# A cross-attention block with a locality-gated mixture of experts: token reads in row tiles of 32x128, another order of the attention steps, and scatters declared independent

## The chip, the cores and the metric

The kernel runs on one core of one Trainium2 chip. The metric is device time in microseconds for one execution. Several runs are timed and their median is compared; one further execution is taken by the hardware profiler, and all views of the profile come from that one.

## The reference

```python
# attention: x (8, 8, 512, 64), state (8, 8, 32, 64)
scores = x @ state^T / sqrt(D);   xread = softmax(scores) @ state     # each token reads 32 states
scores2 = state @ x^T / sqrt(D);  sread = softmax(scores2) @ x        # each state reads 512 tokens
x = concatenate([xread, sread], axis=2)      # then heads joined: (8, 544, 512)
# experts: w1 (8, 512, 1024), w2 (8, 1024, 512)
logits = x @ w_gate;  local_gate = sigmoid(x @ w_local)
for b, s in order:                            # per sequence, token by token
    fresh_e = argmax(logits[b, s])
    e = fresh_e if s == 0 or local_gate[b, s] < 0.5 else prev_e
    prev_e = e
    out[b, s] = softmax(logits[b, s])[e] * (relu(x[b, s] @ w1[e]) @ w2[e])
```

Everything is float32. There are 4352 tokens in all (8 sequences of 512 tokens and 32 states), and each goes through one expert, so the work of the second part is that of 4352 rows through two layers, whichever expert each row chooses.

## The kernel before

The kernel has three stages.

**Attention** goes over 8 batches b. The 8 heads of a batch are held as 4 pairs k in groups of 32 partitions, two halves u, so that the scores of one half are one PSUM bank of 128 partitions (4 heads x 32 states) by 512 tokens. For each (b, u): scores on PE (`sc`), maximum over the tokens on DVE (`mx`), 32x32 transposes on DVE (`tr`), maximum over the states (`mo`), subtraction on POOL (`sb`), exponent on ACT (`ex`), sums (`zh` on POOL, `zs` on DVE), the inverse (`zi`), the shares on POOL (`ml`) and the transposes back on DVE (`tb`), which leave the tile `a`: 128 partitions (4 heads x 32 states) by 512 tokens. A second path makes the state reads: exponents over tokens on ACT (`et`), a turn on PE (`tu`), its copy (`ec`), the products with x (`sr`), their scaling (`st`), and a write to the DRAM tensor `rows` (`ws`). Logits for tokens (`lg`, `lt`) and for states (`rt`, `sl`, `sk`) go to the tile `lt`.

The *token reads* (`vv`, L432) multiply the shares by the states. Here the states of four heads were spread into `sd`, a block-diagonal tile of 128 partitions by 256 columns per (b, u), by four ACT copies (`sd`, L268) over a tile cleared on POOL (L220). A step is one (b, chunk of 128 tokens): two matmuls with a contraction of 128 partitions and 256 columns into one PSUM bank, an ACT copy (`xr`, L438) to an SBUF tile of 128x512, and a write of 256 KB to `rows` (`wr`, L446). There are 32 such steps. The pool `p` of four PSUM banks serves token reads, turns, state reads and logits in turn.

The order of all these steps is written out by hand in the string `STEPS`: each name is a step, its digits the batch and the half or chunk. Every engine executes its instructions in the order in which they are issued there. `go` marks where the list pauses and the routing goes on; at each call of `reads()` inside the routing, the steps up to the next `go` are issued.

**Routing** finds the expert of every token (`choose`, L521 to L527; the step `ch` does batches 0 to 6 at once, and the routing itself does the last batch), carries the choice along each sequence with a scan (L557), counts tokens by expert, and gives each token a slot. ACT makes `less` (L607), `behind` (L612) and `end8` (L619) for DVE on the way. The result is `two` (L716), the first two blocks of tokens, then `tok` and `row` for all blocks. A small POOL DMA (`seen`, L719) reads one element of each batch's rows and so waits for all writes to `rows`. Then POOL gathers the first rows (`y`, L827).

**Experts** handles pairs of blocks (256 tokens of one expert) with a seven-product scheme in both layers, 16 pairs in this data, and 9 small tiles of 32 tokens. For each pair u, PE computes 7 products of the first layer (L1013) and 7 of the second (L1053). POOL gathers the rows of later pairs by quarters (L821), each behind a one-element copy (`tick`, L835) that sets the moment, and scatters the two finished blocks y0 and y1 to the output with indirect DMAs (L996). Both scatters write the tensor `out_dram`. The last pairs are issued by `last`, which branches on the number of pairs found at run time.

Of the kernel before, what the change touches and what calls it, by code (L numbers as in the profile page):

```python
# [150 lines left out]
sc0 kp3 xt11 xt10 mx00 ga kp2 sd3 tr01 xt21 mx01 sd2 mo01 nb0 tr00 et01 sb01 xn0 mo00 wm14 sc1 et00 sb00 ex01  # L151
iv0 tu01 tr11 gl tu00 zh01 ex00 tr10 xt20 ec00 zh00 zs01 mo10 sd0 xn1 zs00 sb10 zi0 ec01 mx11 sd1 sr0 ml01 mo11
ex10 mx10 sc2 ml00 st0 xt30 tb01 rt0 sb11 tb00 sl0 xt31 tr20 lg0 nb1 ex11 zh10 sk0 tr21 vv03 et10 zh11 xt41 zs10
vv00 et11 lt0 mx21 xr03 xt51 zs11 tu11 zi1 xr00 tu10 iv1 ml11 mo21 vv02 xt50 ec10 mo20 ml10 sc3 ec11 tb11 xt40
xr02 mx20 sb21 sr1 tb10 xn2 tr30 sb20 ex21 lg1 mx30 st1 vv12 zh21 ex20 rt1 tr31 nb2 sl1 zh20 et20 vv10 zs21 sk1
lt1 ws1 zs20 et21 tu20 zi2 xt60 mo30 xr10 ml20 sc4 xr12 iv2 mx31 ec20 xn3 ml21 tu21 tb20 vv11 mx41 ec21 nb3 sb30
et30 tb21 sr2 tr40 et31 xt61 lg2 mo31 ex30 tu30 mo40 sb31 st2 sc5 lt2 wr00 xr11 mx40 ec30 zh30 tr41 wr03 tu31
ex31 nb4 zs30 sb40 vv23 et40 mx50 xt70 ec31 mo41 tu40 zh31 ex40 rt2 sr3 sb41 zs31 ws0 xr23 zi3 xn5 et41 iv3 sl2
ml31 mx51 vv22 ex41 sk2 iv4 st3 ml30 tb31 sc6 xr22 rt3 ec40 zh41 tb30 xt71 sl3 zh40 zs41 lg3 tr50 nb5 vv31 wr02
zs40 et50 zi4 vv01 xn4 lt3 xr31 ml40 mo50 sk3 tr51 xr01 vv13 ml41 tb40 et51 vv21 mo51 sb50 xr13 wr10 iv5 vv20  # L160
tb41 xr21 sb51 xn6 mx60 ex50 lg4 mx61 xr20 zh50 tu50 ex51 lt4 tu41 tr60 nb6 ec50 zh51 tu51 zs50 et60 mo60 vv32
wr20 ec51 zs51 sb60 zi5 tu60 ec41 wr23 tr61 sc7 xr32 ml50 wr11 ex60 mo61 sr4 et61 ml51 tb50 wr12 mx71 sr5 sb61
ws2 st4 tb51 ec60 ws3 vv30 tr70 zh60 ex61 xn7 mx70 st5 lg5 zh61 xr30 zs60 tu61 mo70 nb7 et70 vv40 zs61 sb70 zi6
ec61 tu70 lt5 wr22 iv6 xr40 ml61 rt5 sr6 rt4 ex70 tr71 wr40 ec70 ml60 mo71 sl5 et71 wr13 sl4 sk5 tb61 vv41 sb71
st6 wr31 tb60 tu71 zh70 ex71 sk4 iv7 wr32 lg6 rt6 xr41 zs70 zh71 sl6 ec71 lt6 wr21 vv42 zs71 zi7 wr01 sr7 sk6
xr42 ml71 ch0 wr42 vv33 st7 ml70 wr41 vv50 tb71 xr33 wr33 tb70 vv53 xr50 rt7 wr30 lg7 xr53 sl7 lt7 wr53 vv51 sk7
go wr50 vv43 xr51 wr51 go xr43 vv52 wr43 vv61 xr52 ws4 vv60 wr52 xr61 go ws5 xr60 vv62 wr60 go xr62 ws7 wr62
vv71 wr61 vv72 xr71 wr71 vv63 xr72 wr72 vv70 xr63 go wr63 go xr70 wr70 ws6 go vv73 xr73 wr73
# [3 lines left out]
class Attention:  # L172


    def __init__(self, ctx, tc, p, late, xn, xt, st, stt, wgl, wgs, lt, rows, none):
# [14 lines left out]
        self.sttc = [once.tile([P, n, KT, N], F32, name=f"sttc{i}") for i, n in enumerate((1, B - 1))]  # L190
# [3 lines left out]
        self.states_of = once.tile([P, B * G * DH], F32, name="states_of")  # L194
        nc.sync.dma_start(out=self.states_of, in_=st)
        nc.sync.dma_start(out=self.sttc[1], in_=stt[:, 1:])
        nc.sync.dma_start(out=wgs.rearrange("p w k e -> p (w k e)"), in_=wgl)
# [3 lines left out]
        self.sd = late.tile([P, B, G * GD], F32, name="sd", bufs=1)  # L201
# [10 lines left out]
    def clear(self):  # L212
        nc = self.nc
        for z in self.zh:
            nc.vector.memset(z[:, :, N // 2:], 1e-9)
        for z in self.z2:
            nc.vector.memset(z[:, :, 1:], 1e-9)
        nc.gpsimd.memset(self.gl, 0.0)
        nc.gpsimd.memset(self.lt, 0.0)
        nc.gpsimd.memset(self.sd, 0.0)  # L220
        nc.gpsimd.memset(self.none, 0.0)
# [8 lines left out]
    def reads(self):  # L230
# [7 lines left out]
                  sd=self.diagonal, ga=self.gates, gl=self.gates_kept, ch=self.choose, kp=self.keep, wm=self.warmed)  # L238
# [23 lines left out]
    def choose(self, i):  # L262
        self.route.choose(self.lt, 0, B - 1)

    def diagonal(self, k):
        r = slice(32 * k, 32 * k + 32)
        to = self.sd[r].rearrange("p b (g d) -> p b g d", g=G)
        self.nc.scalar.copy(to[:, :, :, DH * k:DH * k + DH],  # L268
                            self.states_of[r].rearrange("p (b g d) -> p b g d", b=B, g=G))

    def load_t(self, b, h):
        x = self.new(self.xp, f"x_t{h}", (b,), [P, KT // 2, S])
        self.nc.sync.dma_start(out=x.rearrange("p k s -> p (k s)"), in_=self.xt[b][:, h * D * 2:(h + 1) * D * 2])

# [4 lines left out]
    def states(self, b):  # L279
        return self.sttc[b > 0][:, b - (b > 0)]  # L280
# [147 lines left out]
    def token_reads(self, b, c):  # L428
        v = self.of["v", b, c] = self.bank()
        for u in range(G):  # L430
            d = slice(u * GD, u * GD + GD)
            self.nc.tensor.matmul(v[:, d], lhsT=self.get("a", b, u)[:, c * P:c * P + P], rhs=self.sd[:, b, d],  # L432
                                  start=True, stop=True)

    def reads_kept(self, b, c):
        xr = self.new(self.late, "xr", (b, c), [P, D], bufs=12)
        v = self.get("v", b, c)
        self.nc.scalar.copy(xr.rearrange("p (k u d) -> p u k d", k=KT, u=G),  # L438
                            v.rearrange("p (u k d) -> p u k d", u=G, k=KT))

    def reads_to_rows(self, b, c):
# [3 lines left out]
        t = b * T + c * P  # L445
        self.nc.sync.dma_start(out=self.rows[t:t + P].rearrange("t q x -> t (q x)"), in_=self.get("xr", b, c))  # L446


class Routing:
# [65 lines left out]
    def choose(self, lt, b0, b1):  # L515
# [5 lines left out]
        nc.vector.memset(lt[0:1, b0:b1, 0, E:E + 1], -1.0)  # L521
        nc.vector.tensor_reduce(self.mx[:, c].rearrange("p c o -> p (c o)"), lf[:, :, :E], axis=AX, op=Alu.max)
        nc.vector.tensor_tensor(self.eq[:, c], lf[:, :, :E], self.mx[:, c].to_broadcast([P, n, E]), op=Alu.is_lt)
        nc.vector.scalar_tensor_tensor(self.eq[:, c], self.eq[:, c], float(2 * E), up.to_broadcast([P, n, E]),
                                       Alu.mult, Alu.add)
        nc.vector.tensor_reduce(self.own[:, c], self.eq[:, c], axis=AX, op=Alu.min)
        nc.vector.scalar_tensor_tensor(self.top[:, c], lf[:, :, E], 0.0, self.own[:, c], Alu.is_lt, Alu.mult)  # L527

    def route(self, bank, lt, slots, reads, rows):
# [12 lines left out]
        self.choose(lt, B - 1, B)  # L542
# [239 lines left out]
def experts(ctx, late, tc, bank, w1, w2, rows, slots, route, routing, out):  # L782
# [35 lines left out]

    def quarter(to, k, i):
# [55 lines left out]
    class Tile:  # L875
# [48 lines left out]
        def scatter(self, y):  # L924
            at = bass.IndirectOffsetOnAxis(ap=slots.row[:, self.k, self.q:self.q + 1], axis=0)
            nc.gpsimd.indirect_dma_start(out=out.rearrange("n (q x) -> (n q) x", q=Q), out_offset=at, in_=y,
                                         in_offset=None, bounds_check=NT * Q - 1, oob_is_err=False)
# [66 lines left out]
    def scatter(b, y):  # L994
        to = bass.IndirectOffsetOnAxis(ap=slots.tok[:, b:b + 1], axis=0)
        nc.gpsimd.indirect_dma_start(out=out, out_offset=to, in_=y, in_offset=None, bounds_check=NT - 1,  # L996
                                     oob_is_err=False)
# [232 lines left out]
```

## Time and profile before

| quantity | value |
|---|---|
| median of 3 runs (lowest to highest) | 550.07 us (545.01 to 551.1) |
| the profiled execution's own time | 546.65 us |
| its span, first to last instruction | 544.9 us |
| mean granted clock of PE | 0.987 |
| busy: PE, DVE, POOL, ACT | 524.6, 382.5, 313.0, 174.0 us |
| bytes moved | 155.48 MB, 285 GB/s on average |
| first expert matmul of PE, last matmul's end | 95.08, 535.15 us |

Busy times are sums over the span; a share says little here because the three stages have different limits. In a line of a timeline, the first number is the start in microseconds from the first instruction, the second the length, then the engine, the line of the kernel, the operation, the output and inputs and the number of instructions; square brackets give idle time before it and what ended that. PEld is PE's weight load. A line of a group gives busy time and the mean of one instruction in ns, and behind the second bar the idle time before the group.

### The profile page before, as it was taken

The page shows a single profiled execution, that of the slowest core. Times are in us where ns is not written, and L with a number is a line of the kernel's source. Part 1 is how long each engine was busy: PE and PEld are TensorE (multiplying, and loading weights), DVE is VectorE, ACT ScalarE, POOL GpSimd, SP SyncE. Part 2 cuts the span into 40 slices and gives each one's busy share as a digit, 9 for nine tenths or more (in the row PEclk, how much of TensorE's full clock was granted, in tenths as well). Part 3 has the DMA queues.
Part 4 walks back from the last instruction along what each step waited for, and adds up shares of the span by engine and source line. Part 5 has one row for each costly group of instructions (what it writes and reads, how often), then busy time and mean ns, then how long its engine had stood idle before and what let it go on. Part 6 is the DMA issues. An engine that isn't in the chain of part 4 may idle for free. (4 is left out here: it accounts for less than half of the span.)

```text
span 544.9 us, 12958 instructions
## 1 busy us (share of the span) xinstructions
PE 524.6 (96%) x4916; PEld 459.3 (84%) x4916; DVE 382.5 (70%) x623; ACT 174.0 (32%) x359; POOL 313.0 (57%) x386
## 2 busy tenths in 40 slices
PE   8799898999999999999999999999999999999992
PEld 2567766989989898989898989899999998999992
DVE  6999876738575667575756658495776777777763
ACT  6788654111313232222222222223222221322230
POOL 7788602655574567565655556446565655445555
PEclk9999998999999999999999999999999999999997
DMA  8999766799989898898989898874748475565742
GB/s 320 410 350 350 294 237 214 275 397 390 377 284 387 299 376 322 327 369 299 375 294 369 293 366 299 320 251 142 259 142 302 134 276 178 216 218 205 248 151 99
DMA packets 49003, 155.48 MB, mean 285 GB/s; under 512 B 6865, under 2 KB 8017, under 8 KB 45602
## 3 DMA queue, kind: packets, MB, share of 16 engines
q1 hardware_dynamic: 41234, 135.78, 68.5%
q0 software_dynamic: 7552, 18.69, 9.6%
q8 instruction: 42, 0.69, 0.5%
q14 instruction: 31, 0.25, 0.1%
q10 hardware_dynamic: 144, 0.07, 0.1%
HBM read 136.68 MB, written 17.89 MB: 284 GB/s over the span
## 5 line engine op out<-in xcount | busy, mean ns | idle before, releaser
L821 POOL DMA_INDIRECT xg<-rows,row x132 | 157.4, 1192 | 29.5 <-issue 27.3
L930 DVE TENSOR_TENSOR a<-a,a 128x1024 f32<-128x1024 f32 x64 | 77.0, 1223 | 31.2 <-DMA a<-in_w_dram 29.8
L1013 PE MATMUL ps<-xt,a 128*128 128x128 f32 x720 | 88.6, 276 | 0.0
L1013 PE MATMUL sum<-xs,a 128*128 128x128 f32 x720 | 87.7, 275 | 0.0
L1013 PEld LDWEIGHTS ps<-xt,a 128*128 128x128 f32 x720 | 84.4, 192 | 2.1 <-issue 1.8
L1013 PEld LDWEIGHTS sum<-xs,a 128*128 128x128 f32 x720 | 84.0, 192 | 0.0
L930 DVE TENSOR_TENSOR c<-c,c 128x1024 f32<-128x1024 f32 x64 | 75.4, 1219 | 3.7 <-DMA c<-in_w_dram 3.2
L1053 PE MATMUL ps<-c,h 128*128 128x256 f32 x312 | 74.7, 382 | 0.0
L1053 PEld LDWEIGHTS ps<-c,h 128*128 128x128 f32 x312 | 58.0, 190 | 10.9 <-issue 3.7
L996 POOL DMA_INDIRECT out_dram<-y,tok x32 | 35.0, 1093 | 52.8 <-issue 16.8
L1053 PE MATMUL ps<-c,hs 128*128 128x256 f32 x256 | 60.5, 379 | 0.0
L1053 PEld LDWEIGHTS ps<-c,hs 128*128 128x128 f32 x256 | 48.6, 190 | 6.6
L1053 PE MATMUL sum<-c,h 128*128 128x256 f32 x200 | 47.2, 379 | 0.0
L930 DVE TENSOR_TENSOR h<-s,s 128x512 f32<-128x512 f32 x15 | 10.4, 693 | 51.5 <-ACT s L1036 48.2
L1053 PEld LDWEIGHTS sum<-c,h 128*128 128x128 f32 x200 | 38.0, 190 | 5.2
L849 DVE STREAM_TRANSPOSE xt<-xg 128x512 f32<-128x512 f32 x32 | 34.2, 1091 | 8.4 <-DMA xg<-rows,row 8.4
L964 ACT COPY sum<-ps 128x256 f32<-128x256 f32 (+1 forms) x31 | 14.3, 460 | 71.1 <-PE ps L1013 49.5
L835 POOL COPY tick<-s 1x1 f32<-1x1 f32 x45 | 15.9, 354 | 36.3 <-ACT s L1036 36.3
L835 POOL COPY tick<-r 1x1 f32<-1x1 f32 x41 | 17.2, 419 | 30.5 <-ACT r L1058 22.9
L432 PE MATMUL p<-sd,a 128*128 128x256 f32 x128 | 32.1, 390 | 0.2 <-ACT xr L438 0.2
L1058 ACT ACTIVATE r<-sum,prob 128x256 f32<-128x256 f32 x32 | 15.1, 473 | 52.0 <-PE sum L1053 49.5
L1053 PE MATMUL sum<-c,hs 128*128 128x256 f32 x128 | 30.2, 379 | 0.0
(230 smaller groups left out, 757.8 us busy)
## 6 DMA issues: line engine op xcount, KB each, us to landing
a<-in_w_dram SPq DMA_DIRECT2D x68, 512.0 KB
c<-in_w_dram SPq DMA_DIRECT2D x68, 512.0 KB
at<-in_w_dram SPq DMA_DIRECT2D x18, 1024.0 KB
ct<-in_w_dram SPq DMA_DIRECT2D x18, 1024.0 KB
x_t<-in_xt_dram SPq DMA_DIRECT2D x16, 512.0 KB
x_n<-in_xn_dram SPq DMA_DIRECT2D x8, 1024.0 KB
rows<-xr SPq DMA_DIRECT2D x32, 256.0 KB
xg<-rows,row POOLq DMA_INDIRECT x132, 5.7
```

The lines of the kernel that those rows point to most:

```text
L432: self.nc.tensor.matmul(v[:, d], lhsT=self.get("a", b, u)[:, c * P:c * P + P], rhs=self.sd[:, b, d], start=True, stop=True)
L821: nc.gpsimd.indirect_dma_start(out=to.rearrange("p x k -> p (x k)"), out_offset=None, in_=rows.rearrange("n q x -> (n q) x"), in_offset=ba ...
L835: nc.gpsimd.tensor_copy(tick, value)
L849: nc.vector.transpose(to.rearrange("p k (i t) -> p k i t", i=Q), xgs_[u % 2][:, b].rearrange("p i x k -> p k i x"))
L930: nc.vector.tensor_tensor(out, a, b, op=op)
L964: nc.scalar.copy(y, x)
L996: nc.gpsimd.indirect_dma_start(out=out, out_offset=to, in_=y, in_offset=None, bounds_check=NT - 1, oob_is_err=False)
L1013: nc.tensor.matmul(to[:, m * P:m * P + P], lhsT=w[:, j, m * P:m * P + P], rhs=x[:, j, :], start=begin and m == 0 and j == 0, stop=(m == FK ...
L1053: nc.tensor.matmul(to, lhsT=x[:, m, :], rhs=w[:, m, :], start=begin and m == 0, stop=(m == FK // 2 - 1), skip_group_check=True)
L1058: nc.scalar.activation(to, t, Act.Copy, scale=p)
```

## The change

Six things change.

1. A token-read step is now a whole batch. The tile `sd`, its memset and its four copies go; the states are used as loaded, 32 partitions and 64 columns for each head. Each head pair k has a PSUM bank of its own, so one step takes all four banks of the pool `p`; it issues 32 matmuls of 32 partitions x 128 stationary columns by 64 moving columns. Four ACT copies of 128x512, one for each bank, fill one SBUF tile, and one DMA writes 1 MB to `rows`.
2. The order in `STEPS` is new throughout.
3. The choice of batches 0 to 6 is issued as five steps, `ca` to `ce`, with other steps between them, behind the last logits.
4. The initial loads are split: the states of batch 1 (`la`) before the others (`lb`).
5. The scatters to the output are declared independent of one another, for pairs and for small tiles.
6. In the last pairs, the fourth quarter of the gather that goes with the second layer is issued only behind the branch, when another pair follows.

```diff
 STEPS = """   (the end of the list)
-st6 wr31 tb60 tu71 zh70 ex71 sk4 iv7 wr32 lg6 rt6 xr41 zs70 zh71 sl6 ec71 lt6 wr21 vv42 zs71 zi7 wr01 sr7 sk6
-xr42 ml71 ch0 wr42 vv33 st7 ml70 wr41 vv50 tb71 xr33 wr33 tb70 vv53 xr50 rt7 wr30 lg7 xr53 sl7 lt7 wr53 vv51 sk7
-go wr50 vv43 xr51 wr51 go xr43 vv52 wr43 vv61 xr52 ws4 vv60 wr52 xr61 go ws5 xr60 vv62 wr60 go xr62 ws7 wr62
-vv71 wr61 vv72 xr71 wr71 vv63 xr72 wr72 vv70 xr63 go wr63 go xr70 wr70 ws6 go vv73 xr73 wr73
+sl3 tu61 mo71 et71 ws5 sk3 zs70 sb71 wr3 ex61 iv7 tu71 iv6 ec61 rt5 zh61 sl5 ex71 sr6 sk5 ec71 zs61 zh71 zi6 sr7
+ml61 zs71 st6 zi7 ws6 rt6 ml60 sl6 st7 tb61 ws7 sk6 rt7 vv2 ml71 tb60 ml70 tb71 xr23 xr21 tb70 xr20 xr22 sl7 lg6
+wr2 sk7 lg7 lt6 ca lt7 cb vv6 cc cd ce xr63 go xr62 xr60 go xr61 vv5 wr6 xr53 xr51 go xr50 xr52 go wr5 vv4 xr43
+xr41 xr40 xr42 vv7 wr4 go go xr73 xr72 xr70 go xr71 wr7
...
-        for u in range(G):
-            d = slice(u * GD, u * GD + GD)
-            self.nc.tensor.matmul(v[:, d], lhsT=self.get("a", b, u)[:, c * P:c * P + P], rhs=self.sd[:, b, d],
-                                  start=True, stop=True)
+        v = self.of["v", b] = [self.bank().rearrange("p (c u d) -> p c u d", c=SC, u=G) for k in range(KT)]
+        for c in range(SC):
+            for u in range(G):
+                for k in range(KT):
+                    r = slice(32 * k, 32 * k + 32)
+                    self.nc.tensor.matmul(v[k][:, c, u, :], lhsT=self.get("a", b, u)[r, c * P:(c + 1) * P],
+                                          rhs=self.states_of[r, b, u, :], start=True, stop=True)
...
+    def reads_kept(self, b, k):
+        xr = self.new(self.late, "xr", (b,), [P, SC, KT, G * DH], bufs=3)
+        self.nc.scalar.copy(xr[:, :, k, :], self.get("v", b)[k].rearrange("p c u d -> p c (u d)"))
...
+        self.nc.sync.dma_start(out=self.rows[t:t + S].rearrange("(c t) q x -> t c (q x)", c=SC),
+                               in_=self.get("xr", b).rearrange("p c k x -> p c (k x)"))
...
+    def apart(scatter):
+        tc.declare_no_dep(scatter.ins, group="scatters", reason="a token has one slot, so scatters write other rows")
+        tc.add_to_no_dep_group("scatters", scatter.ins)
...
+        rest = gets[1]
+        if not late:
+            calls = iter(range(NP))
+            gets[1] = lambda value: rest(value) if next(calls) < Q - 1 else None
...
-        pair(u, u + 1 < NP, waiting=waiting, late=False)
+        rest = pair(u, u + 1 < NP, waiting=waiting, late=False)
         if u + 1 < NP:
             with tc.If(pairs > u + 1):
+                rest()
                 last(u + 1)
```

## The prediction

> **What bounds the kernel now.** I read the busy time by stage first, then the line of time inside each stage, then the groups, then the chain that ended last.
>
> Busy time in five stages: columns are the stretch, its length, busy time and instructions of PE, PEld, DVE, ACT and POOL, granted clock, DMA share, GB/s.
>
> ```profile
> 8.05:57.26 49.21, 44.63 (x913) 30.18 (x915) 46.80 (x110) 41.28 (x93) 39.23 (x50) 1.00 0.98 374
> 57.26:69.45 12.19, 10.84 (x211) 8.92 (x200) 10.58 (x33) 6.77 (x16) 6.37 (x7) 1.00 0.75 276
> 69.45:95.08 25.63, 22.81 (x169) 16.40 (x168) 18.12 (x58) 13.05 (x31) 2.96 (x3) 0.92 0.65 227
> 95.08:535.15 440.07, 440.07 (x3619) 402.14 (x3616) 300.04 (x405) 109.27 (x210) 253.23 (x311) 1.00 0.79 284
> 535.15:544.90 9.75, 0.00 (x0) 0.00 (x0) 2.75 (x3) 0.00 (x0) 4.51 (x4) 0.65 0.23 76
> ```
>
> Attention, 8.05 to 69.45: DVE works 57.4 of 61.4 us, so DVE sets it, not PE. Routing, 69.45 to 95.08: a chain of small steps over DVE, PE and ACT. Experts, 95.08 to 535.15: PE without a gap at the full clock; the pairs with a small tile repeat every 28.73 us. Nothing there can be gained by an edit that takes no matmul away, and the change takes none. What is left to move is the start of the experts and the 9.75 us after PE's last matmul.
>
> The line of time gives the links that I use:
>
> ```profile
> 9.55 1.19 PEld L289 LDWEIGHTS p<-wgs,sttc 64*32 64x32 f32 x128 [1.29 <-DMA wgs<-in_wg_dram]
> 61.93 0.35 DVE L363 RECIPROCAL z<-z 128x32 f32<-128x32 f32 x1
> 62.20 1.10 PE L390 MATMUL p<-x_n,e 128*32 128x64 f32 x64
> 62.42 2.26 POOL L367 TENSOR_TENSOR e<-e,z 128x512 f32<-128x512 f32 x2 [1.00 <-DVE lt L521]
> 69.28 0.17 DVE L527 SCALAR_TENSOR_TENSOR top<-lt,own 128x5 bf16<-128x5 f32 x1
> ...
> 78.49 0.15 ACT L619 COPY end<-ps 8x2 f32<-8x2 f32 x1 [0.17 <-PE ps L617]
> 78.99 0.22 DVE L627 TENSOR_SCALAR past<-iof,end 8x23 bf16<-8x23 f32 x1
> 83.42 0.83 POOL L719 DMA_DIRECT2D seen<-rows  x1 [18.74 <-DMA rows<-xr]
> 85.03 0.95 PEld L710 LDWEIGHTS <-inp 128*128 128x128 bf16 x16 [0.15 <-DVE inp L686]
> 88.17 0.16 DVE L716 TENSOR_TENSOR two<-high,ps 128x2 int32<-128x2 f32 x1
> 89.39 1.17 POOL L827 DMA_INDIRECT y<-rows,two  x1 [5.13 <-DMA a<-in_w_dram]
> ```
>
> The last choice (L527) ends at 69.45, ACT's copy end8 (L619) lets DVE go on at 78.99, `two` is ready at 88.33, the gather of the first rows goes out at 89.39 and PE begins at 95.08. POOL's `seen` shows when the last row has landed: 83.4, five us ahead of need.
>
> The groups by shape, for the part that is rewritten:
>
> ```profile
> L432 PE MATMUL p<-sd,a 128*128 128x256 f32 x128 | 32.1, 390 | 0.2 <-ACT xr L438 0.2
> L390 PE MATMUL p<-x_n,e 128*32 128x64 f32 x512 | 8.9, 220 | 3.4 <-DMA x_n<-in_xn_dram 2.9 <-issue 0.5
> L438 ACT COPY xr<-p 128x512 f32<-128x512 f32 x32 | 18.6, 586 | 9.5 <-PE p L432 8.6 <-ACT others L634 0.9
> ```
>
> The tail, POOL in order of time, and then the piece of the chain that lies between the two scatters:
>
> ```profile
> 535.04 1.02 POOL L996 DMA_INDIRECT out_dram<-y,tok  x1 [0.30 <-issue]
> 536.03 0.81 POOL L835 COPY tick<-y 1x1 f32<-1x1 f32 x1
> 537.00 1.80 POOL L821 DMA_INDIRECT xg<-rows,row  x1 [0.16 <-issue]
> 540.07 1.02 POOL L996 DMA_INDIRECT out_dram<-y,tok  x1 [1.27 <-DMA out_dram<-y,tok]
> ```
>
> ```profile
> 535.04 4.20 DMA out_dram<-y,tok
> ```
>
> **The change, part by part.** *Scatters (tail).* The second scatter of the last pair waits for the first to land and has a tick and a gather before it. Both go. Its data (L1080) is ready at 535.66, so it starts at 535.04 + 1.02 + 0.30 = 536.36 in place of 540.07: -3.7. The two 256 KB scatters then travel together; scatters took 3.2 to 10.2 us to land in this trace, so I give 0.3 back: **-3.4**, bounds -2.0 and -3.7. The same wait vanishes in the other pairs, where PE's 440 us cover it (POOL idled up to 7.8 us there and PE not at all). The deferred gather goes out after the branch, still some 15 us ahead of its transpose: nothing. Without that cover DVE's L849 would wait, as it does now for 8.4 us in all.
>
> *Work taken off PE, ACT and POOL in attention.* Gone: the 3.5 us memset of `sd`, four ACT copies of 1.04, and most of the 32.1 us of L432. DVE waited for PE 2.2 us in the whole stage, 1.0 of it really for the load of the second x_t; ACT and POOL are below it. So nothing directly: DVE's own 57.4 us cover it.
>
> *The new order on DVE.* The instructions are the same; only waits can change. Head: the second batch's x_t comes after the same bytes, so its wait (12.4 to 13.35) stays. x_n of batch 0 moves behind three x_t halves, and the maxima of batch 2 come before it is used: 0 to +0.9. Middle: 1.2 us of small waits, of which some may close. End: now POOL makes the last shares (62.42 to 64.68) while DVE runs the 3.4 us choice of batches 0 to 6 (62.24 to 65.73). The change puts that choice behind the last logits, so its cover is gone: the four shares of 1.05 follow one another on POOL and DVE has a 0.6 us transpose between them, three waits of 0.4; and the sums of the second half of batch 6 wait 0.7 for subtract, exponent and halves. From the last score transpose to the last choice I count 2.7 us of waits in place of 1.6: +1.1. Together I take **+0.6** (end +1.1, half a us back in the middle), bounds -2.8 (all 4.0 us of idle gone but the 1.2 of the load) and +2.0.
>
> *Token reads as a serial chain.* Let P be PE's time for one batch: 64 loads and 64 passes of 64 columns, in four row tiles. A batch takes all four banks of the pool, so the next cannot begin before the four copies (0.54 apart) are done. In the order issued, 17 of 32 copies were done by the last reciprocal before; after, 12. Batches 5, 4 and 7 now stand, one after the other, ahead of the matmul of `ends` on PE and, 5 and 4, of `less` on ACT. From the end of the last choice c: the exponent waits for DVE (0.5) and takes 0.5, the fourth copy of batch 6 ends at c + 1.6; batch 5: 0.2 + P + 0.25 + 2.1; batch 4 the same; batch 7: 0.2 + P; `ends` and end8 0.7. With P = 1.1: c + 10.9, where now it is 78.99 - 69.45 = 9.5. **+1.3**, and three times every us that P is longer. DVE waits there, and behind it the slots, `two`, the gather and PE's first matmul.
>
> P itself no row shows. Below: 1.10 us for the 64 records of L390, four column tiles side by side (0.93 without start-up). Above: loads that do not overlap, 0.95 / 16 = 59 ns each (L710), 64 of them 3.8 us. L289 decides: 128 loads of 32 columns in 1.19 us are 9.3 ns each, less than a quarter of 59, so loads into different tiles do run together. I take 1.1.
>
> The Trainium skill (TensorE: Matmul & The Clock Gate, LDWEIGHTS) says that a load's time goes by columns and that 32x128 costs as much as 128x128, which speaks against four times as many loads. No run here shows it for row tiles; taken alone it would give the serial 3.8 us and the slow case below.
>
> PE's clock: granted 0.50 from 88 to 90 us although PE shows busy, after two us of four-column matmuls. With fewer matmuls in routing that can come earlier; P would be 2.2 and the sum 3.3 us more.
>
> *Rows.* 32 writes of 256 KB become 8 of 1 MB on SP, the last after the last copy (c + 13.2) instead of at 81.32 = c + 11.9; 0.75 MB more at 380 GB/s adds 2 us to the 2.1 that it took to land: c + 17.4. `two` comes at c + 20: covered by 2.6 us, beyond which every us counts. The first expert's loads stand behind it on SP and meet the gather: **+0.3**, bounds 0 and 1. On SP the row writes of five batches move behind all loads of x, which then land earlier; that is part of the lower bound on DVE, and 22 issues of 0.33 us fewer on a queue that nobody waits for are worth nothing. Four more warming matmuls lie in PE's idle 14.3 to 17.1, the extra load on SP behind full DMA queues: nothing.
>
> Sum: -3.4 + 0.6 + 1.3 + 0.3 = -1.2. The profiled execution took 546.65 (span 544.9 and 1.75 around it) and would take 545.4; the median of the runs is 550.07, 3.4 above it, so I forecast **548.9**. Runs of before spread over 1.1%, so about 1% (5.5 us) is what can be told from no change; this is within.
>
> **The rivals.** *Row tiles that do not run together.* P = 3.8, from serial loads; the chain is 3 x 2.7 = 8.1 longer: 548.9 + 8.1 = 557.0. For it: 128 columns a load, no row of this form. Against it: L289. Slower at all from P = 1.5, by over 1% from P = 3.3.
>
> *The order closes DVE's waits.* -2.8 on DVE, P = 0.93 (chain +0.8), no collision, tail -3.7: -5.7, 544.4. For it: the idle is there and PE, ACT and POOL are relieved. Against it: the lost cover at the end, which I could follow link by link.
>
> *The scatters gain nothing,* because the second meets the first on its way: +3.4, 552.3. Against it: the 4.2 us are a wait and not a transfer.
>
> **How the numbers follow.** Forecast 0.44, with its own range 546 to 552.5; serial tiles, or a cold clock added to other losses, 0.27; waits closed 0.25; scatters without gain 0.04, which is within 1% too. So faster by over 1% 0.25, within 0.48, slower 0.27. The range 543.5 to 557.5 takes in both rivals' times with a little beyond.
>
> **What would show it.** Tail: the last two scatters 1.3 us apart, some 6 us from PE's end to the span's. Token reads: 64 records in about 1.1 us. Routing: DVE's step behind end8 (now L627) at c + 10.9. DVE: idle before the last transposes; the last choice near 70. Experts: 440 us as before. I am wrong if PE's first expert matmul comes before 95 or after 101, or if the stretch of experts itself changes.

## The result, and the profile after

The changed kernel takes 575.74 us (median of 4 runs, 572.47 to 578.24) against 550.59 us (4 runs, 545.01 to 552.39): the ratio is 1.0471, with a 95% interval of 1.0374 to 1.0569. Here and below a ratio leaves out executions more than 1.5% above the fastest of the same kernel, while a median takes in all. The kernel is slower by 25 us, and the forecast of 548.9 us with its range up to 557.5 is wrong.

The profiled execution took 578.24 us, its span is 576.4 us. Its busy time by stage, columns as in the prediction (length, PE, PEld, DVE, ACT, POOL, granted clock, DMA share, GB/s):

```profile
8.04:57.26 49.22, 39.88 (x956) 25.45 (x954) 43.77 (x98) 31.18 (x75) 36.42 (x47) 0.90 0.93 342
57.26:77.71 20.45, 17.11 (x373) 14.81 (x373) 13.03 (x44) 9.70 (x24) 9.05 (x10) 0.68 0.50 190
77.71:113.59 35.88, 31.70 (x341) 24.90 (x337) 18.21 (x57) 14.96 (x36) 3.11 (x3) 0.64 0.55 193
113.59:569.69 456.10, 452.00 (x3619) 404.43 (x3616) 300.51 (x405) 109.42 (x210) 248.97 (x311) 1.00 0.76 275
569.69:576.40 6.71, 0.00 (x1) 0.00 (x0) 2.75 (x3) 0.00 (x0) 1.73 (x1) 0.77 0.16 54
```

The last choice now ends at 77.71, PE's first expert matmul starts at 113.59, its last ends at 569.69. Before, these were 69.45, 95.08 and 535.15. Two things stand out against the stages of before: the granted clock is 0.64 to 0.90 up to the experts (it was 1.00, and 0.92 in routing), and PE is idle for 4 us in the experts, where it had no gap. By links of the chain:

| link | before | after | difference | forecast |
|---|---|---|---|---|
| last choice ends | 69.45 | 77.71 | +8.3 | +0.6 |
| from there to DVE's step behind end8 | 9.5 | 19.4 | +9.9 | +1.3 |
| from there to the first expert matmul | 16.1 | 16.4 | +0.3 | +0.3 |
| experts | 440.1 | 456.1 | +16.0 | 0 |
| PE's end to the end of the span | 9.75 | 6.7 | -3.0 | -3.4 |

The sum is +31.5 us, which is the difference of the two spans. The medians are 25 us apart: the profiled execution is the slowest of the four of after, and that of before lies below its median.

Some token reads on PE in order of time: one in attention, three in routing (seven matmuls of the first of these stand outside its row of 57), then the matmul of `ends` and the DVE step that waits for its copy.

```profile
53.02 2.01 PE L434 MATMUL p<-states_of,a 32*128 32x64 f32 x64
81.37 3.46 PE L434 MATMUL p<-states_of,a 32*128 32x64 f32 x57 [0.16 <-ACT xr L439]
86.66 4.24 PE L434 MATMUL p<-states_of,a 32*128 32x64 f32 x64
91.62 5.14 PE L434 MATMUL p<-states_of,a 32*128 32x64 f32 x64 [0.72 <-ACT xr L439]
97.15 0.23 DVE L641 TENSOR_SCALAR past<-iof,end 8x23 bf16<-8x23 f32 x1 [3.32 <-ACT end L633]
```

A read takes 2.01 us where the clock is 1.00 and 3.5 to 5.1 us in routing. The same view cut at the steps of the granted clock shows why:

```profile
30.56:40.80 10.24, 9.89 (x117) 5.70 (x116) 8.25 (x18) 6.89 (x17) 8.32 (x11) 0.50 1.00 389
57.87:68.11 10.24, 8.82 (x142) 7.29 (x146) 5.57 (x19) 6.00 (x15) 4.73 (x7) 0.50 0.64 244
74.93:102.24 27.31, 24.62 (x278) 19.95 (x279) 14.30 (x53) 9.64 (x26) 0.00 (x0) 0.50 0.50 185
```

For 47.8 us ahead of the experts PE has half its clock, although it counts as busy for nine tenths of that time. The first stretch begins as the first read ends (28.04 to 30.57), and in the third 18.4 of PE's 24.6 busy us are reads. Ahead of the second PE had also been idle, from 56.49 to 59.29, so that stretch need not come from the reads alone. Who waited for whom in attention (total, times, longest):

```profile
DVE lt L425 <- PE p L421: 5.8, 4, 3.3
DVE nb L314 <- PE s L306: 5.0, 4, 2.8
PE p L389 <- issue: 2.8, 1, 2.8
PE p L421 <- issue: 1.7, 1, 1.7
```

The same view of before has 0.8 us for the first row and 0.2 us for the second. DVE, which set attention before, now waits for PE, and twice PE itself waited for nothing that the trace shows ("issue"). The tail does what was forecast. Its last scatter starts as soon as its data is there:

```profile
567.14 1.03 POOL L1015 DMA_INDIRECT out_dram<-y,tok  x1 [0.30 <-DVE y L1092]
570.57 1.73 POOL L1015 DMA_INDIRECT out_dram<-y,tok  x1 [2.41 <-DVE y L1099]
```

The 16 us in the experts lie in the pairs with a small tile. One of them, in order of time:

```profile
163.75 1.01 POOL L945 DMA_INDIRECT out_dram<-yt,row  x1 [0.30 <-issue]
163.89 1.01 PEld L923 LDWEIGHTS ps<-at,xtt 128*32 128x32 f32 x23
163.89 3.63 PE L923 MATMUL ps<-at,xtt 128*32 128x256 f32 x32
165.06 1.33 POOL L840 DMA_INDIRECT xgt<-rows,row  x1 [0.30 <-issue]
165.48 0.15 PEld L923 LDWEIGHTS ps<-at,xtt 128*32 128x32 f32 x4 [0.57 <-issue]
166.21 0.17 PEld L923 LDWEIGHTS ps<-at,xtt 128*32 128x32 f32 x4 [0.58 <-issue]
```

The first 23 weight loads come as before, then four at a time with 0.57 us between them, again for no reason that the trace shows; the 32 matmuls take 3.63 us, where before they took 1.93. Nearly all of the 16 us is here: 13.8 in these matmuls of the tiles' first layer (10.0 busy and 3.8 idle), some 2 in those of their second. POOL issued the tile's scatter 0.14 us ahead of them. Before, it came behind them, because it waited for the pair's scatters to land.

### The profile page after: what moved, and what is told of

Read it like the earlier page. It is cut to its first block, busy times and chain, and to the rows that moved or that the text cites. A ratio compares the mean times of both kernels' runs of the same rounds, so it can differ in the third digit from the quotient of the medians.

```text
span 576.4 us, 13666 instructions
## 1 busy us (share of the span) xinstructions
PE 547.1 (95%) x5302; PEld 471.3 (82%) x5302; DVE 379.9 (66%) x623; ACT 168.9 (29%) x355; POOL 302.5 (52%) x383
## 4 chain that ended last, share of the span: by engine, by line
PE 82%; issue 2%; DVE 1%; ACT 1%; DVEq 0%
PE ps L1072 22%; PE ps L1032 19%; PE sum L1032 14%; PE sum L1072 12%; PE ps L923 5%; PE ps L935 3%; PE ps L1116 3%; PE ps L724 2%; PE p L434 2%; PE ps L551 1%; ACT xr L439 0%; DVE a L949 0%; PE ps L875 0%; PE sum L551 0%; DVE oh L584 0%
## 5 line engine op out<-in xcount | busy, mean ns | idle before, releaser
L840 POOL DMA_INDIRECT xg<-rows,row x131 | 151.4, 1156 | 36.3 <-issue 36.1
L949 DVE TENSOR_TENSOR a<-a,a 128x1024 f32<-128x1024 f32 x64 | 76.8, 1221 | 15.3 <-DMA a<-in_w_dram 13.9
L1072 PEld LDWEIGHTS ps<-c,h 128*128 128x128 f32 x312 | 58.0, 190 | 10.9 <-issue 3.7
L854 POOL COPY tick<-r 1x1 f32<-1x1 f32 x41 | 11.6, 282 | 86.5 <-ACT r L1077 83.2
L1015 POOL DMA_INDIRECT out_dram<-y,tok x32 | 37.6, 1174 | 26.1 <-DVE y L1099 14.4
L434 PEld LDWEIGHTS p<-states_of,a 32*128 32x128 f32 x512 | 28.2, 271 | 5.3 <-ACT xr L439 3.6
L434 PE MATMUL p<-states_of,a 32*128 32x64 f32 x512 | 30.1, 365 | 1.2 <-ACT xr L439 0.9
L923 PE MATMUL ps<-at,xtt 128*32 128x256 f32 x288 | 27.4, 385 | 3.8 <-issue 2.4
```

The lines of the kernel that those rows point to most:

```text
L434: self.nc.tensor.matmul(v[k][:, c, u, :], lhsT=self.get("a", b, u)[r, c * P:(c + 1) * P], rhs=self.states_of[r, b, u, :], start=True, stop ...
L840: nc.gpsimd.indirect_dma_start(out=to.rearrange("p x k -> p (x k)"), out_offset=None, in_=rows.rearrange("n q x -> (n q) x"), in_offset=ba ...
L854: nc.gpsimd.tensor_copy(tick, value)
L923: nc.tensor.matmul(hps[SQ * g:SQ * g + SQ, :], lhsT=self.x_t[:, j, :], rhs=a[:, j, :, g], start=(j == 0), stop=(j == KT - 1))
L949: nc.vector.tensor_tensor(out, a, b, op=op)
L1015: apart(nc.gpsimd.indirect_dma_start(out=out, out_offset=to, in_=y, in_offset=None, bounds_check=NT - 1, oob_is_err=False))
```

## Experiments

Two theories at the start. *A:* the time before the experts goes to the row-tile reads, by their length on PE and by the clock that they bring down; the time in the experts goes to scatters that now meet the tiles' matmuls. *B:* the reads are innocent, the new order makes the chain long, and the experts suffer from something else, such as PE's longer program. The runs come from five chips; every ratio is against the kernel before on the same chip, and that kernel's own median went from 545.45 to 550.92 us between chips.

### First chip: the parts apart

scatters_alone: the kernel before with parts 5 and 6 of the change and nothing else.

```diff
-        nc.gpsimd.indirect_dma_start(out=out, out_offset=to, in_=y, in_offset=None, bounds_check=NT - 1,
-                                     oob_is_err=False)
+        apart(nc.gpsimd.indirect_dma_start(out=out, out_offset=to, in_=y, in_offset=None, bounds_check=NT - 1,
+                                           oob_is_err=False))
...
+            calls = iter(range(NP))
+            gets[1] = lambda value: rest(value) if next(calls) < Q - 1 else None
```

> The kernel before with the independent scatters and the gather deferred behind the branch, and nothing else of the change. Theory A: a small tile's scatter, no longer held back by the landing of the pair's scatter, goes out some 0.3 us ahead of the tile's first-layer matmuls and slows their issue; 2 us a tile, 8 tiles of 9. The stretch of experts 452 to 456 us in place of 440, the tail 6.7 us in place of 9.75, the time some 10 to 13 us above the kernel before. Rival R: the experts are slow in the changed kernel because PE's program is longer and its code comes later, not because of scatters. Experts 440 us, tail 6.7, the time 3 us below the kernel before.

Measured: 560.03 us, ratio 1.0191 (1.0146 to 1.0236). First expert matmul at 94.55, experts 456.7 us, tail 6.65. So the loss in the experts comes with the scatters (the deferred gather concerns only the last pairs, which have no tile), without any other part of the change.

scatters_undone: the changed kernel without those two parts.

```diff
-            apart(nc.gpsimd.indirect_dma_start(out=out.rearrange("n (q x) -> (n q) x", q=Q), ...))
+            nc.gpsimd.indirect_dma_start(out=out.rearrange("n (q x) -> (n q) x", q=Q), ...)
...
```

> The changed kernel with the scatters dependent on one another again and the last gather where it was. Theory A: first expert matmul at 113 to 114 us as in the changed kernel, experts 440 us, tail 9.8, the time some 563 to 566, 12 below the changed kernel. Rival R: experts still 456 us; only the tail comes back, the time 3 us above the changed kernel.

Measured: 566.49 us, ratio 1.0267 (1.0201 to 1.0332). First expert matmul at 111.6, experts 444.3 us. The two halves of the loss separate, as A has it: the tiles' first layer is back at 17.4 us, as in the kernel before. Some 4 us above 440 remain, most of them in the tiles' second layer (20.0 us busy and 0.8 idle, where before it took 17.6).

wide_reads: the changed kernel with the old form of the reads.

```diff
-        v = self.of["v", b] = [self.bank().rearrange("p (c u d) -> p c u d", c=SC, u=G) for k in range(KT)]
...
+        v = self.of["v", b] = [self.bank() for c in range(SC)]
+        for c in range(SC):
+            for u in range(G):
+                d = slice(u * GD, u * GD + GD)
+                self.nc.tensor.matmul(v[c][:, d], lhsT=self.get("a", b, u)[:, c * P:c * P + P], rhs=self.sd[:, b, d], ...)
```

> The changed kernel with the token reads as they were: a block-diagonal tile, two matmuls of 128 partitions by 256 columns for each chunk, in the new order, four banks a batch. Theory: the row tiles are what makes PE slow and lowers its granted clock (0.50 from 75 to 102 us), and that delays DVE's last choice too. Then the clock stays at 1.00 in attention, the last choice ends at 70 to 73 us, the first expert matmul comes at 95 to 99, the experts stay slow by 16 us, the time is 557 to 562. Rival: the new order itself makes the choice late and the chain behind it long; last choice at 75 or later, first expert matmul at 105 or later, the time 567 or more.

Measured: 576.24 us, ratio 1.0485 (1.0424 to 1.0546). Last choice at 79.97, first expert matmul at 110.83. My expectation failed: as a whole the old form is no better in this order. But the clock behaves as A has it. While the same three reads stand at the same place of the chain, PE keeps its full clock:

```profile
80.00:102.60 22.60, 18.83 (x113) 12.96 (x114) 14.55 (x48) 12.43 (x33) 0.21 (x1) 1.00 0.61 210
94.69 0.23 DVE L648 TENSOR_SCALAR past<-iof,end 8x23 bf16<-8x23 f32 x1 [1.90 <-ACT end L640]
```

A wide read of a whole batch takes 3.72 us at the full clock. From the last choice to DVE's step behind end8 the chain takes 14.7 us with three of those: 5.2 more than before, 4.7 less than the 19.4 with row tiles at half clock. Most of that is lost again before: beside scatters_undone, which has the row tiles on the same chip, the last choice comes 3.6 us later (76.4 there) and the first expert matmul 0.8 sooner. In attention the clock is not the row tiles' alone, since this run has it at half for some 10 us between 20 and 60 us. Both parts count: an order that puts whole batches into the chain, and a form that loses the clock. (The four block-diagonal copies of ACT, which I placed, cost DVE 1.9 us as well; so this run does not price the order alone.)

rows_in_turn: the same matmuls, one row tile after the other.

```diff
-        for c in range(SC):
-            for u in range(G):
-                for k in range(KT):
+        for k in range(KT):
+            for c in range(SC):
+                for u in range(G):
```

> The changed kernel with the 64 matmuls of a token read in another order: all 16 of one row tile, then the next row tile, in place of four tiles side by side. If loads into different row tiles overlap, this takes the overlap away: a batch goes from 2.0 us at the full clock to 3 or more, and the time grows by 4 to 8 us. If they run one after the other already, a batch stays at 2.0 us (4 to 5 at half clock) and the time within 3 us of the changed kernel.

Measured: 626.11 us, ratio 1.1401 (1.133 to 1.1472); a read takes up to 11.5 us at half clock in place of 4.2:

```profile
119.23 11.53 PE L434 MATMUL p<-states_of,a 32*128 32x64 f32 x64
```

So row tiles side by side do overlap, by a factor of 2.7 (11.53 / 4.24, both at half clock). The Trainium skill (TensorE: Matmul & The Clock Gate, Packing small matmuls) gives 3.07 for four row tiles with 512 columns; with 64 columns this case comes near it, with 2.7. My rival of tiles that do not run together is refuted.

### Second chip: place, form, order, clock

tile_scatter_late: scatters_alone, with the tile's scatter meant to be issued later.

```diff
-            strassen(u, others, gets[0], waiting)
+            strassen(u, others, gets[0], waiting[:2])
...
+        for results in waiting[2:]:
+            results()
```

> The kernel before with the independent scatters and the deferred gather, as scatters_alone, but each small tile's scatter is issued on POOL behind the gather of the next tile, some 2.3 us later, when the tile's first-layer matmuls are nearly over. Theory: it is the scatter's coincidence with the tile's matmuls that costs 2 us a tile. Then the tile's 32 first-layer matmuls take 1.9 us again, experts 440 to 444 us, tail 6.7, the time 546 to 550, at or 3 us below the kernel before. Rival: independent scatters cost PE the same wherever they lie; experts 452 or more, the time 556 or more.

Measured: 543.75 us, ratio 0.9958 (0.9933 to 0.9983), experts 440.5 us. The edit proved to be empty: a pair has only two results waiting, and both stayed where they were, so these are the instructions of scatters_alone in the same order, on another chip. There the same program lost 16 us, here nothing. The loss in the tiles belongs to some chips (no chip was used a second time, so a cause that lasts only as long as one stay on a chip is not excluded).

plain_tile_writes: scatters_alone with a plain write to a scratch tensor in place of the tile's scatter; the kernel leaves out the small tiles' rows of the output.

```diff
-            apart(nc.gpsimd.indirect_dma_start(out=out.rearrange("n (q x) -> (n q) x", q=Q), out_offset=at, in_=y, ...))
+            nc.gpsimd.dma_start(out=spare[self.i * P:self.i * P + P], in_=y)
```

> As scatters_alone, but each small tile's result goes out by a plain DMA of the same 64 KB, issued by POOL at the same place, to a scratch tensor; the rows of the small tiles in the output are left out. If any write issued there slows PE, the experts stay at 454 to 457 us and the time at 558 to 561. If it is the indirect form (POOL working out an address for every row) they come back to 440 to 444 us and the time to 547 or so.

Measured: 544.75 us, ratio 0.9968 (0.9941 to 0.9995), experts 441.1 us. Inconclusive, since on this chip the indirect form loses nothing either.

rows_old_order: row-tile reads in the order of before, a batch at a time, with the scatters dependent as before (one stretch of the order).

```diff
-ml00 st0 xt30 tb01 rt0 sb11 tb00 sl0 xt31 tr20 lg0 nb1 ex11 zh10 sk0 tr21 vv03 et10 zh11 xt41 zs10
-vv00 et11 lt0 mx21 xr03 xt51 zs11 tu11 zi1 xr00 tu10 iv1 ml11 mo21 vv02 xt50 ec10 mo20 ml10 sc3 ec11 tb11 xt40
+ml00 st0 xt30 tb01 rt0 sb11 tb00 sl0 xt31 tr20 lg0 nb1 ex11 zh10 sk0 tr21 et10 zh11 xt41 zs10 et11 lt0 vv0 xr00
+xr01 xr02 xr03 mx21 xt51 zs11 tu11 zi1 tu10 iv1 ml11 mo21 xt50 ec10 mo20 ml10 sc3 ec11 tb11 xt40 mx20 sb21 sr1 tb10
```

> The token reads in row tiles, four banks a batch, in the order of before: each batch's read stands where its first or second chunk stood, behind the next point at which all banks are free; choice in one step, scatters and last gather as before. Theory 1: the row tiles are the cause, by their time on PE and the clock they bring down, whatever the order: the granted clock falls to 0.50 for 20 us or more before 100 us, the first expert matmul at 104 or later, the time 559 or more. Theory 2: the new order is the cause: last choice at 69 to 72, first expert matmul at 95 to 99, the time 549 to 554.

Measured: 573.62 us (four executions, 565.42 to 575.45; the profile is of one at 573.99), ratio 1.0415 (1.0319 to 1.0511). First expert matmul at 120.9, half clock for 58 us ahead of 108, experts 440.8 us. In favour of theory 1, the row tiles, but not clean: the last choice comes only at 90.6, and DVE waited 7.2 us for ACT at one step and 17.8 for PE at four. I take it that whole-batch reads with their four copies in one piece stand ahead of DVE's inputs, which the old order was not made for; no run separates that.

warm_reads: dense matmuls ahead of every read.

```diff
+        for i in range(6):
+            self.nc.tensor.matmul(v[0].rearrange("p c u d -> p (c u d)"), lhsT=self.zero[:, :P], rhs=self.zero,
+                                  start=True, stop=True)
```

> The changed kernel with six dense matmuls on zeros (128 by 512, bf16, 0.24 us each at the full clock) ahead of the 64 of every token read, into a bank that the read overwrites. If the clock falls because row-tile matmuls hardly count as work, the dense ones hold it up: half-clock stretches before 112 us shrink from 47.7 us to under 25, a read takes 1.5 + 2.0, the first expert matmul comes at 106 to 111, the time 568 to 573. If the clock falls for another reason (waits between the reads), they only add 1.5 to 2.9 us a batch: first expert matmul 118 or later, 580 or more.

Measured: 553.58 us, ratio 1.0131 (1.009 to 1.0172), faster than I had expected. In the chain the clock stays full:

```profile
80.00:90.00 10.00, 8.38 (x184) 6.40 (x187) 4.62 (x23) 4.35 (x11) 0.00 (x0) 1.00 0.61 223
88.77 2.08 PE L437 MATMUL p<-states_of,a 32*128 32x64 f32 x64
```

Half clock for 17 us in place of 47.8, the reads in the chain at 2.0 to 2.3 us, DVE's step behind end8 13.9 us after the last choice in place of 19.4, first expert matmul at 106.5, experts 438.8 us. More work on PE shortens the chain, because it keeps the clock; no theory of waits or of program length says that. (Of the 22 us to the time on record, some 17 are the chip, on which the tiles lose nothing.)

### Third chip: the change and its parts side by side

changed_again: the changed kernel as it is.

> The changed kernel as it is, once more, to have it beside the others on the same chip. scatters_alone lost 16.6 us in the experts; the same instructions in the same order, run as tile_scatter_late on another chip (the edit there changed no instruction's place), lost 0.4. So the loss in the small tiles may belong to the chip. If it does, the experts here take either 440 to 444 us (time 560 to 563, ratio 1.025 to 1.03) or 454 to 458 (573 to 578); if it belongs to the program, 456 again. The first expert matmul at 111 to 115 us either way.

Measured: 560.33 us against 546.69 us, ratio 1.0245 (1.0213 to 1.0276). Last choice at 72.81, first expert matmul at 108.46, and the experts without a gap:

```profile
108.46:548.59 440.13, 440.13 (x3619) 402.20 (x3616) 299.33 (x405) 109.40 (x210) 254.08 (x311) 1.00 0.79 285
```

So on a chip without the loss in the tiles, the change costs 13.6 us, and all of it lies ahead of the experts. The issue waits of attention are 0.9 us here in place of 4.5, and the last choice comes 4.9 us sooner. The chain behind it takes 19.4 us, as on the record's chip.

tile_after: the edit that tile_scatter_late missed.

```diff
-            strassen(u, others, gets[0], waiting)
+            strassen(u, others, gets[0], waiting[:1] if tile else waiting)
...
         between()
+        for results in waiting[1:] if tile else ():
+            results()
```

> The kernel before with the independent scatters and the deferred gather, each small tile's scatter moved on POOL behind the next tile's gather, so that it starts some 2.3 us after the tile's first matmul in place of 0.3 us ahead of it. On a chip where independent scatters slow the tiles: experts 440 to 446 us in place of 456 if the coincidence is the cause, 450 or more if not. On a chip where they don't: 440 us. The tail 6.7 us, the time 2 to 3 us below the kernel before if nothing else is lost.

Measured: 544.35 us, ratio 0.9946 (0.9921 to 0.9971), experts 440.5 us. On this chip it can't tell.

last_apart: independent scatters in the last seven pairs alone, on the kernel before.

```diff
+        if free:
+            apart(done)
...
-                scatter(2 * u, ys[0])
+                scatter(2 * u, ys[0], not late)
```

> The kernel before with independent scatters in the last seven pairs alone, which have no small tile, and the deferred gather there. Theory: all that the edit can gain is the wait of the last scatter, 3.0 us; tail 6.7 us, experts 440 us on any chip, ratio 0.993 to 0.997. Rival: the two scatters slow each other, or PE, in those pairs too; ratio 1.00 or above.

Measured: 542.92 us, ratio 0.9921 (0.9898 to 0.9945). Experts 438.8 us, tail 6.7. This is 0.8% below the kernel before, and below the changed kernel.

warm_half: three dense matmuls in place of six.

```diff
-        for i in range(6):
+        for i in range(3):
```

> The changed kernel with three dense matmuls ahead of each token read in place of six. If three are enough to hold the clock, a read takes 0.7 + 2.0 us and the first expert matmul comes at 103 to 106 us, 1 to 3 us sooner than with six (106.5). If they are not, half-clock stretches of 25 us or more come back before 112 us and it comes at 109 to 116 us. The stretch of experts as in changed_again.

Measured: 555.13 us, ratio 1.0187 (1.0131 to 1.0243), first expert matmul at 104.4 against 108.46 for changed_again beside it. The clock is at 1.00 from 28 to 78 us and at 0.50 for the 17.1 us behind that: three hold it in attention, not in the chain, where two of the three reads take 3.7 us and the link to DVE's step takes 16.4. The last choice is at 72.5, beside 72.8 for changed_again: a full clock in attention does not bring it forward here.

### Fourth and fifth chip: the loss in the tiles

> The same kernel as scatters_alone, again. If the loss in the small tiles belongs to the chip, the stretch of experts is either 439 to 445 us or 454 to 458; a value between would speak for a cause that changes from run to run.

> The same kernel as tile_after, again, beside scatters_alone_2 on one chip. If scatters_alone_2 loses 10 us or more in the experts, this tells whether a scatter that starts behind the tile's matmuls avoids it: experts 440 to 446 us if the coincidence is the cause, above 450 if independent scatters slow PE wherever they lie. If scatters_alone_2 loses nothing, both are at 439 to 445 and the question stays open.

Measured: scatters_alone_2 560.11 us, experts 457.0; tile_after_2 562.07 us, experts 456.3 (one run each). This chip has the loss, and it stays although the tile's own scatter now starts about 0.9 us behind the tile's first matmul. In its place POOL issues the next tile's gather 0.3 us ahead of the tile. So the scatter need not lie ahead. In most tiles it still starts while the matmuls run, but in the second tile the loads stop, after 31 of 32 (148.58 + 1.45 = 150.03), before it starts:

```profile
148.58 1.45 PEld L909 LDWEIGHTS ps<-at,xtt 128*32 128x32 f32 x31
148.96 0.95 POOL L826 DMA_INDIRECT xgt<-rows,row  x1 [0.30 <-issue]
150.21 1.07 POOL L931 DMA_INDIRECT out_dram<-yt,row  x1 [0.30 <-issue]
150.53 0.11 PEld L909 LDWEIGHTS ps<-at,xtt 128*32 128x32 f32 x1 [0.51 <-issue]
```

So it is not the scatter as such; the next tile's gather goes with a stop too.

tile_waits: POOL waits for the tile's first layer before it issues either.

```diff
-            strassen(u, others, gets[0], waiting)
+            strassen(u, others, gets[0], waiting[:1] if tile else waiting)
...
                 tile.one()
+                nc.gpsimd.tensor_copy(tick, tile.h[0:1, 0, 0:1])
+                for results in waiting[1:]:
+                    results()
```

> The same kernel as scatters_alone, as a marker of the chip: experts 439 to 445 us on a chip without the loss, 454 to 458 on one with it.

> scatters_alone, but POOL waits for the tile's first layer (a one-element copy of its result) before it issues the tile's scatter and the next tile's gather, so no indirect DMA is issued between 0.6 us ahead of the tile's matmuls and their end. On a chip with the loss: if what costs is an indirect DMA, scatter or gather, issued just ahead of those matmuls (tile_after_2 still had the next tile's gather 0.3 us ahead of them), the 32 matmuls take 1.55 us from first to last start again and the experts 440 to 446 us. If it is the scatter of the pair on its way, 4 us older, 454 to 458 remain. On a chip without the loss both are 440.

Measured on one chip: scatters_alone_3 557.34 us, experts 453.0; tile_waits 548.13 us, experts 443.7 (one run each). The groups of the tiles' first layer, scatters_alone_3 first, then tile_waits:

```profile
L909 PE MATMUL ps<-at,xtt 128*32 128x256 f32 x288 | 24.8, 384 | 4.1 <-issue 3.6
```

```profile
L909 PE MATMUL ps<-at,xtt 128*32 128x256 f32 x288 | 17.4, 382 | 0.0
```

17.4 us and no idle time is what the kernel before has. So on such a chip the tile's scatter and the next tile's gather, issued beside a tile's matmuls, slow the issue of those. Not every indirect DMA there does. In all runs with the loss the first tile takes 1.93 us, although a gather starts 0.09 to 0.62 us ahead of it, and so does the second tile of last_apart_2, on the fifth chip, with a gather at the moment of its first matmul:

```profile
146.62 1.93 PE L909 MATMUL ps<-at,xtt 128*32 128x256 f32 x32
146.62 1.37 POOL L826 DMA_INDIRECT xg<-rows,row  x1 [0.16 <-issue]
```

The last tile, with a scatter 0.3 us ahead and no gather behind it, takes 2.6 to 2.8 us; most of those between, with both, 3.6 to 4.2. What else it takes for a loss is not shown.

> The same kernel as last_apart, on what may be another chip. Its pairs with tiles keep the dependent scatters, so on a chip with the loss it should lose nothing: experts 439 to 444 us, tail 6.7, ratio 0.990 to 0.997. If it loses in the experts there, ratio 1.00 or above.

Measured on that chip: 546.63 us against 549.96 us, ratio 0.9943 (0.9909 to 0.9977), experts 442.6 us. The version without independent scatters beside tiles is free of the loss in the tiles' first layer (17.4 us) and faster on both chips where it ran. Its experts still take 3.8 us more than on the third chip, with 19.3 us in place of 17.6 in the tiles' second layer. The chips differ in the kernel before as well: its median is 550 to 551 us on the three with the loss, 545.5 and 546.7 on the two without.

## Why the prediction was wrong

- **P, the time of a batch's read (1.1 us), was the first step that failed.** I let L289 decide, whose loads are 32 columns wide and four side by side. For row tiles of 128 columns, 64 loads and passes take 2.0 us at the full clock. The tiles do run together, as I had argued, but for four tiles the pair of load and pass costs 31 ns and not 17.
- **The clock was the second, and the larger.** I gave a cold clock 3.3 us, as a side case that fewer matmuls in routing might bring. In the chain it came from the reads themselves and doubled P; it began to fall at 30.6 us in the middle of attention. The formula of the chain, c + 10.9 with P = 1.1 and three us for every us of P, came near. With P = 2.0 it gives 13.6, and warm_reads measured 13.9 (its dense matmuls need one bank only and run while the other copies are made); with the 3.46, 4.24 and 5.14 us of after it gives 10.9 + 12.84 - 3.3 = 20.4, and 19.4 were measured. That is good to 1 us at best, since the first of these rows has 57 of 64 matmuls and they may hold waits for banks. By this estimate, of the +9.9, 1.3 are the serial chain that I had priced, 2.7 the true P, and the rest, some 6, the clock.
- **"So nothing directly: DVE's own 57.4 us cover it" was the third.** I took PE in attention as relieved. Whole-batch reads, some of them at half clock, stand ahead of scores and logits on PE, and DVE waited for PE 10.8 us at two steps of the scores and token logits, where I had read 2.2 for the whole stage. On the record's chip 4.5 us of issue waits come with it; without them changed_again still had its last choice at 72.8, 3.4 us later than the profile of before, where I had +0.6. Beside it on the same chip, last_apart and tile_after, with the attention of before, had theirs at 70.2 and 71.2, so some 2 us are the change and the rest is the chip or the execution. That it is the clock is not shown: warm_half had a full clock there and gained 0.3 us.
- **The scatters beside the tiles were costed at nothing, and that failed on some chips.** "PE's 440 us cover it" named the cover, but PE itself was hit: 16 us in the record, some 17 on the first chip and the fourth, 13 on the fifth, none on the second and third. The trace of before showed the tile's scatter some 4 us behind the tile's first matmul; I did not ask what it would meet if it came earlier.
- **The tail was right** (-3.4 forecast, -3.0 measured, and last_apart gains 3.8 us at the median on one chip and 3.3 on another), though its two scatters are 3.4 us apart and not 1.3, since the first now goes out ahead of PE's end and the second waits for its data, and so was the rest of routing (+0.3).
- **The rivals.** Serial row tiles came nearest with 557.0 us, by the wrong mechanism: rows_in_turn shows that tiles overlap. Its price was too low as well, taken from loads of bf16: in turn a read took 11.53 us at half clock, where 3.8 at the full clock would make 7.6. The effect that I priced for it, P near 3.8 in the chain, is what the half clock made. Neither the gain of closed waits nor a loss of the scatters' gain occurred.

Left open: how an indirect DMA of POOL comes to slow the issue on PE, why some that lie beside a tile do not, and what sets the chips apart. How much of the late last choice is the order and how much the reads was not separated cleanly either; both wide_reads and rows_old_order carried costs of their own.

## What to carry to other kernels

Count a small matmul's weight load and pass together, at the clock that a stretch of such matmuls will be granted: a form that takes 2.0 us in place of 3.72 at the full clock can lose all of it at half. A wait that is removed lets its instruction run earlier, so look at what stands at that earlier place on the other engines; take the wait out only where it is the last thing (here seven pairs of sixteen). And before a loss is explained, see whether the same program has it on another chip, and whether every place that has the supposed cause has the loss.

## What the runs showed of the hardware

- Row-tile matmuls of 32 x 128 by 64 columns do not hold PE's clock. In the changed kernel it stood at 0.50 for 27.3 us with PE 90% busy, three quarters of that with reads; with wide matmuls at the same place it stayed at 1.00, and six dense matmuls of 0.24 us ahead of each read brought it back in the chain. The Trainium skill (TensorE: Matmul & The Clock Gate, The HAM clock gate) puts the fall down to idle windows of some 3.4 us. The lengths here, 10.24 and 27.31 us, are multiples of 3.41, but in the longer one PE was idle for 2.7 us in all: here busy in the profile was not busy for the clock.
- On some chips, PE's issue falls to four loads and four matmuls in 0.73 us for some 2 us, when POOL issues a small tile's scatter and the next tile's gather beside a run of small matmuls (0.3 us ahead of it and 1 us behind its start); a gather 0.1 to 0.6 us ahead of the first tile cost nothing on the same chips. It shows in the tiles, at 60 ns for a load and its matmul (1.93 us for 32); in the changed kernel the large products, at 112 ns in the first layer (1.79 us for 16) and 216 in the second, ran without idle time.
